# Seven half-size products for the second FFN layer of the last three token tiles, and a residue-first attention output

## The chip, the cores and the metric

The kernel runs on one core of a Trainium2 chip. The metric is device time in microseconds (us). Before the change three runs took 296.37, 297.34 and 298.47 us; the median, 297.34 us, is the time that the change is compared with. Five engines work beside each other, each in the order of its own instruction list, and wait for each other by semaphores: TensorE (PE for its matmuls, PEld for its weight loads), VectorE (DVE), ScalarE (ACT), GpSimd (POOL) and SyncE (SP). SP and POOL mainly issue DMAs here.

## The reference

A masked attention (8 batches, 8 heads, 576 positions, head size 64) feeds a feed-forward layer with squared ReLU over 8 x 576 = 4608 tokens.

```python
mask_plain = (rel >= 0) & (rel < window)                                             # heads 0-3
mask_dil = (rel >= 0) & (rel < window * dilation) & (rel % dilation == 0)            # heads 4-7
attn = softmax(where(mask, scale * q @ k.T, -1e9));  attn_out = attn @ v             # window 32, dilation 4
x = attn_out.transpose(0, 2, 1, 3).reshape(4608, 512)
h = np.maximum(x @ w_in, 0.0)                                                        # w_in 512 x 2048
out = h * h @ w_out                                                                  # w_out 2048 x 512
```

## The kernel before

All matmuls take bf16 operands and add up in float32. The attention output is kept transposed in `xT`, 128 channels on the partitions and four blocks of channels (`KT`), in a ring of four batches. Positions are held by residue modulo 4 (`RES`), since the dilated heads look only at positions of their own residue: within a batch the 576 columns stand as 4 residues x 144.

The FFN goes over the tokens in tiles: four tiles of 256 tokens, then seven of 512, which this text numbers 2 to 8 (tile t begins at token 512 t). `ffn_groups` gives the PE work of a tile as a list of small functions. The first half, `g1`, is the first layer: for each of the 16 blocks of 128 hidden features (`NF`) four matmuls over the channel blocks (L971), 128 x 128 weights against 512 columns of `xT`, into one PSUM bank of the pool `ps_f` (four banks, used in turn; the profile calls them `pf`). ACT then takes the ReLU from the bank into `h2T` (L984) and DVE squares it in place (L987). The second half, `g2`, is the second layer: for each of the four blocks of 128 tokens sixteen matmuls (L1027) with a block of `h2T` as the weights and 512 columns of `w_out` streaming; a copy takes the bank to `osb` (L1033, ACT as a rule), and `store` issues it to DRAM on SP's queue (L941). `store` cuts a block of 128 rows wherever a residue ends, so a block goes out in one to three pieces. In the very last block the columns are cut 384 + 128, so that the last copy and the last store are short.

`h2T` is a fresh 512-token buffer for each tile, from a pool of two.

The attention of a batch is laid between the groups of the FFN, with an order written by hand: `PROGRAM` for the first batches, and for the later ones a list `steps` of (group, order, batch, code), with the group number g at which a step is issued. A 512-token tile has 32 groups (`G`), 16 of g1 and 16 of g2. For batch 7, the last, two visits of PE remain in tile 6: after its group 15 (scores of two head pairs, and the products with v of the two others) and after its group 23 (products with v of the last two). Around them ACT takes the exponentials (code E, L730), DVE multiplies by the mask (L732) and adds neighbouring pieces (L735, L744), ACT forms the reciprocal row sums as exp(-ln d) (codes L and X, L698 to L713), and DVE multiplies the result into `xT` (L716, L720). After that, tiles 7 and 8 hold FFN work alone.

Loads of q, k and v go over POOL's queue; `rb[0..2]` are the staging buffers of q and k. `rb[0]` and `rb[2]` are last used by batches 2 and 3.

Of the kernel before, what the change touches and what calls it, by code (L numbers as in the profile page):

```python
# [12 lines left out]
RES = 4  # L13
# [50 lines left out]
def kernel(  # L64
# [9 lines left out]
    nc = tc.nc  # L74
# [3 lines left out]
    NTOK = B * S  # L78
# [30 lines left out]
    h2_pool = ctx.enter_context(tc.tile_pool(name="h2", bufs=2))  # L109
# [26 lines left out]
    rb = [{nm: const.tile([(80, P, 80)[i], 2 * H * RES * D], bf16, name=f"{nm}b{i}") for nm in "qk"} for i in range(3)]  # L136
# [9 lines left out]


    v_rows = [t[:, 0:2, :, :].rearrange("p e i c -> p (e i c)").rearrange("p (e i d) -> p e i d", e=NE, d=D) for t in vbd]
    q_both = qT[:, :, :, :]
    k_both = kbd[:, 0:2, :, :].rearrange("p e i c -> p (e i c)").rearrange("p (i h t) -> p i h t", i=NB, h=NE)  # L150
    ends = [
# [205 lines left out]
    def byr(ap):  # L357
        return ap.rearrange("p (r m) -> p r m", r=RES)
# [165 lines left out]
    def batch1(code: str):  # L524
# [140 lines left out]
        else:  # L665
            e = int(code[1])
            es = (e, e + 1) if part == 0 else (e,)
            if what == "l":
                two["r", e] = rec = r_pool.tile([P, 576], f32, name="rec")
                for x, e in enumerate(es):  # L670
                    ds = two["o", e, part][1]
                    to = rec[:, w * x : w * x + w]
                    if len(ds) == 1:
                        nc.scalar.activation(to, ds[0], ACT.Ln)
                        continue
                    to = to.rearrange("p (c j m) -> p j c m", c=2, j=2)
                    for j, d in enumerate(ds):
                        nc.scalar.activation(to[:, j, :, :], d.rearrange("p (c m) -> p c m", c=2), ACT.Ln)
            else:
                rec = two.pop(("r", e))[:, 0 : w * len(es)]  # L680
                nc.scalar.activation(rec, rec, ACT.Exp, scale=-1.0)
                t0 = S % RING + RES * m0
                for x, e in enumerate(es):
                    o, _ = two.pop(("o", e, part))
                    nc.vector.tensor_tensor(out=xT[:, e, t0 : t0 + w], in0=o, in1=rec[:, w * x : w * x + w], op=ALU.mult)

    def natural_step(b: int, code: str):
        what, e = code[0], int(code[1])
# [21 lines left out]
        elif what == "X":  # L710
            o, _, rest = op.pop((b, e))
            rec = recs.pop((b, e))
            nc.scalar.activation(rec[:, :], rec[:, :], ACT.Exp, scale=-1.0)  # L713
            t0 = b * S % RING
            tok = byr(xT[:, e, t0 : t0 + S])
            nc.vector.tensor_tensor(out=tok[:, :, 16:M], in0=byr(o[:, :]), in1=byr(rec[:, 0:512]), op=ALU.mult)  # L716
            for g, rows in enumerate(sides) if rest[0][0] is not rest[0][1] else [(0, slice(0, P))]:
                if rest[0][0] is not rest[1][0]:
# [49 lines left out]
    def first_step(code: str):  # L768
# [128 lines left out]
        elif what == "D":  # L897
            dms = first.pop(("D", e, part))
            for x, (dd, rh) in enumerate(dms):
                nc.tensor.matmul(  # L900
                    dd, ones[:, :], rh, start=(x == 0 and y0 == 0), stop=(x == len(dms) - 1), skip_group_check=True
                )
        else:
            n = 512 if part == 0 else w
            if what == "L":
                first["X", e, part] = rec = r_pool.tile([P, 576], f32, name="rec")
                nc.scalar.activation(rec[:, 0:n], first["P", e, part][1][:, 0:n], ACT.Ln)
            elif what == "X":
                rec = first["X", e, part][:, 0:n]
                nc.scalar.activation(rec, rec, ACT.Exp, scale=-1.0)  # L910
            else:
                o, rec = first["P", e, part][0][:, 0:n], first.pop(("X", e, part))[:, 0:n]
                to = xT[:, e, RES * m0 : RES * m0 + n]
                if part == 0:
                    to = xT[:, e : e + 2, 0:w]
                    o, rec = [x.rearrange("p (e n) -> p e n", e=2) for x in (o, rec)]
                nc.vector.tensor_tensor(out=to, in0=o, in1=rec, op=ALU.mult)

    def attention_steps(b: int, base: int, at):
# [6 lines left out]
        return out  # L926


    def store(osb, pos: int, c0: int, c1: int, cuts=None):

        x = 0
        while x < P:
            b, y = divmod(pos + x, S)
            part = int(y >= RES * MN[0]) if b in PARTED else 0
            w = MN[part] if b in PARTED else M
            r, m = divmod(y - RES * MS[part], w)
            n = min(P - x, w - m)
            row = b * S + RES * (MS[part] + m) + r
            at = cuts(n) if cuts else (c0, c1)
            for y0, y1 in zip(at, at[1:]):  # L940
                nc.sync.dma_start(out[row : row + RES * (n - 1) + 1 : RES, y0:y1], osb[x : x + n, y0:y1])  # L941
            x += n

    def ffn_groups(tk0: int, nt: int):

        early = NT <= tk0 <= 3 * NT
        h2 = h2_pool.tile([P, NF, NT], bf16, name="h2T")
        per = NT // nt  # L950
        kts = (2, 0, 3, 1) if tk0 > 3 * NT else (2, 3, 1, 0) if tk0 == 2 * NT else (0, 1, 2, 3) if tk0 == 0 else (2, 3, 0, 1)
        cur, acc = {}, {}

        half = nt // 2
        over = tk0 // RING != (tk0 + nt - 1) // RING
        assert not over or (tk0 + half) % RING == 0

        def mm1(u, ks):
            if u not in acc:
                acc[u] = ps_f.tile([P, NT], f32, name="pf")  # L960
            for x in range(per):
                f = per * u + x
                piece = max(y for y in range(len(w_in_sb)) if w_cuts[y] <= P * f)
                c0 = 512 * (f // 4) + f % 4 - w_cuts[piece]
                for kt in ks:
                    t0 = tk0 % RING
                    to, rhs = acc[u][:, nt * x : nt * x + nt], xT[:, kt, t0 : min(t0 + nt, RING)]
                    if over:
                        to = to.rearrange("p (a t) -> p a t", a=2)
                        rhs = xT[:, kt, :].rearrange("p (a t) -> p a t", t=half)[:, 0 : t0 // half + 1 : t0 // half, :]  # L970
                    nc.tensor.matmul(  # L971
                        to,
                        w_in_sb[piece][:, kt, c0 : c0 + 509 : 4],
                        rhs,
                        start=(kt == kts[0] and x == 0),
                        stop=(kt == kts[-1] and x == per - 1),
                        skip_group_check=True,
                    )
            if ks[-1] != kts[-1]:
                return  # L980
            hv = h2[:, per * u : per * u + per, 0:nt]

            def relu():
                nc.scalar.activation(hv, acc[u][:, :].rearrange("p (x n) -> p x n", x=per), ACT.Relu)  # L984

            def square():
                nc.vector.tensor_tensor(out=hv, in0=hv, in1=hv, op=ALU.mult)  # L987

            def floor():
                nc.vector.tensor_scalar(  # L990
                    out=hv, in0=acc[u][:, :].rearrange("p (x n) -> p x n", x=per), scalar1=0.0, scalar2=None, op0=ALU.max
                )

            if tk0 == 0 and u < 2:
                held.append((floor if u else relu, square))
            else:
                relu()
                square()

        def g1(i):  # L1000
            if i < 2 and tk0 < NT or i < 6 and tk0 == 0:
# [17 lines left out]
        def g2(m, part):  # L1019
# [11 lines left out]
            if f1 == NF:  # L1031
                osb = osb_pool.tile([P, DM], f32, name="osb")
                (nc.vector.tensor_copy if last and part == 1 or tk0 == 3 * NT // 2 else nc.scalar.copy)(osb[:, c0:c1], cur[m][:, c0:c1])  # L1033
                pos = tk0 + (P * m + half) % nt if over else tk0 + P * m
                if tk0 == NTOK - NT and m in (0, 2):
                    store(osb, pos, c0, c1, lambda n: (c0, DM // 2, c1) if m == 0 or n > P // 2 else (c0, c1))
                else:
                    store(osb, pos, c0, c1)
# [77 lines left out]
    def cross_all(b):  # L1116
        for part in range(2):
            for nm in "kq":
                cross(b, nm, part)

    def run(code):
        if code == "y":
# [181 lines left out]
```

## Time and profile before

| what | value |
|---|---|
| median of three runs | 297.34 us (296.37 to 298.47) |
| span of the profiled execution, first to last instruction | 294.1 us |
| busy: PE / PEld | 286.2 us (97%) / 165.8 us (56%) |
| busy: ACT / DVE / POOL | 187.2 us (64%) / 155.5 us (53%) / 123.2 us (42%) |
| PE in the first layer (L971) | 127.6 us |
| PE in the second layer (L1027) | 126.0 us |
| tile 6 in the span | 205.08 to 234.91 us |
| tile 7 | 234.91 to 262.54 us |
| tile 8, then the last copies and stores | 262.54 to 294.1 us |

Of the profiled execution the profile gives the span; its own time as a run isn't recorded beside it. The median of the timed runs is 3.2 us above the span: what lies before the first and behind the last instruction of the span, and the difference between one execution and another. In the rows below, times such as "start us" count from the span's start, "mean ns of one" is the recorded length of one instruction (matmuls overlap in the array, so the distance from start to start is what a matmul costs), and the arrow in brackets names what an engine waited for.

### The profile page before, as it was taken

The page shows a single profiled execution, that of the slowest core. Times are in us where ns is not written, and L with a number is a line of the kernel's source. Part 1 is how long each engine was busy: PE and PEld are TensorE (multiplying, and loading weights), DVE is VectorE, ACT ScalarE, POOL GpSimd, SP SyncE. Part 2 cuts the span into 40 slices and gives each one's busy share as a digit, 9 for nine tenths or more (in the row PEclk, how much of TensorE's full clock was granted, in tenths as well). Part 3 has the DMA queues.
Part 4 walks back from the last instruction along what each step waited for, and adds up shares of the span by engine and source line. Part 5 has one row for each costly group of instructions (what it writes and reads, how often), then busy time and mean ns, then how long its engine had stood idle before and what let it go on. Part 6 is the DMA issues. An engine that isn't in the chain of part 4 may idle for free.

```text
span 294.1 us, 7899 instructions
## 1 busy us (share of the span) xinstructions
PE 286.2 (97%) x3213; PEld 165.8 (56%) x3241; DVE 155.5 (53%) x452; ACT 187.2 (64%) x381; POOL 123.2 (42%) x208
## 2 busy tenths in 40 slices
PE   8999999999999999999999999999999999999994
PEld 6689647859555554555455545554554455445443
DVE  2785224647779566685659465947454245004300
ACT  6888545887667774988567656766676476127411
POOL 8686266847626965776763696000000000000000
PEclk9999999999999999999999999999999999999999
DMA  8999999999999999999999698012101210121022
GB/s 120 199 188 214 203 225 197 193 169 190 162 230 141 140 157 199 138 159 171 179 176 116 97 170 144 2 37 73 36 2 39 71 38 0 37 74 33 0 71 71
DMA packets 84211, 35.75 MB, mean 122 GB/s; under 512 B 53600, under 2 KB 79424, under 8 KB 84176
## 3 DMA queue, kind: packets, MB, share of 16 engines
q0 software_dynamic: 49056, 18.49, 56.5%
q1 hardware_dynamic: 34976, 16.67, 28.0%
q8 instruction: 25, 0.41, 0.6%
q10 hardware_dynamic: 144, 0.10, 0.1%
q14 instruction: 10, 0.08, 0.1%
HBM read 37.50 MB, written 9.44 MB: 160 GB/s over the span
## 4 chain that ended last, share of the span: by engine, by line
PE 93%; ACT 1%; issue 1%; DMA 1%; DVE 1%; POOL 0%; ACTq 0%; POOLq 0%
PE pf L1027 42%; PE pf L971 41%; PE po L369 2%; PE pa L369 2%; PE pf L369 1%; DMA kb<-in_k_dram 1%; ACT h2T L984 1%; PE pa L794 1%; PE pd L369 1%; PE pf L846 1%; DVE h2T L987 1%; PE po L764 1%; PE pa L564 0%; DVE qT L335 0%; PE po L884 0%
## 5 line engine op out<-in xcount | busy, mean ns | idle before, releaser
L971 PE MATMUL pf<-xT,w_in 128*128 128x512 bf16 (+1 forms) x697 | 127.6, 340 | 0.4
L1027 PE MATMUL pf<-w_out_sb,h2T 128*128 128x512 bf16 (+2 forms) x571 | 126.0, 373 | 1.6 <-issue 0.6
L984 ACT ACTIVATE h2T<-pf 128x512 bf16<-128x512 f32 x143 | 83.9, 600 | 32.3 <-PE pf L971 32.0
L971 PEld LDWEIGHTS <-w_in 128*128 128x128 bf16 x704 | 78.0, 113 | 46.3 <-issue 0.3
L987 DVE TENSOR_TENSOR h2T<-h2T 128x512 bf16<-128x512 bf16 x144 | 60.0, 424 | 61.5 <-ACT h2T L984 59.6
L1027 PEld LDWEIGHTS <-h2T 128*128 128x128 bf16 x592 | 56.1, 98 | 63.9
L321 POOL DMA_DIRECT2D vbd<-in_v_dram x80 | 43.5, 560 | 23.6 <-DMA kb<-in_k_dram 9.7
L1033 ACT COPY osb<-pf 128x512 f32<-128x512 f32 (+1 forms) x34 | 19.5, 574 | 50.5 <-PE pf L1027 50.5
L175 POOL DMA_DIRECT2D qb<-in_q_dram x19 | 13.7, 722 | 8.3 <-DMA xx<-qb 4.6
L713 ACT ACTIVATE rec<-rec 128x576 f32<-128x576 f32 x24 | 16.4, 683 | 0.7
L175 POOL DMA_DIRECT2D kb<-in_k_dram x19 | 13.3, 698 | 5.8 <-DMA w_in<-in_moe_w_in_dram 1.9
L197 POOL DMA_DIRECT2D vbd<-in_v_dram x16 | 11.0, 687 | 8.9 <-DMA kb<-in_k_dram 5.3
L730 ACT ACTIVATE pt<-pa 128x384 bf16<-128x384 f32 (+1 forms) x26 | 11.7, 498 | 4.5 <-DVE xT L720 3.8
L307 POOL DMA_DIRECT2D vd<-in_v_dram x20 | 12.0, 615 | 3.2 <-PE pa L369 2.1
L313 POOL DMA_DIRECT2D vbd<-in_v_dram x20 | 12.0, 618 | 3.2 <-PE pf L369 1.9
L716 DVE TENSOR_TENSOR xT<-pf,rec 128x512 bf16<-128x512 f32 x11 | 7.6, 692 | 10.5 <-ACT rec L713 10.5
L716 DVE TENSOR_TENSOR xT<-po,rec 128x512 bf16<-128x512 f32 x13 | 9.0, 691 | 6.5 <-ACT rec L713 6.3
L732 DVE TENSOR_TENSOR pt<-pt,mask_n 128x384 bf16<-128x384 bf16 (+1 forms) x20 | 7.2, 374 | 8.6 <-ACT pt L730 8.5
L732 DVE TENSOR_TENSOR pt<-pt,mask_f 128x384 bf16<-128x384 bf16 x24 | 8.4, 355 | 6.1 <-ACT pt L730 5.9
L369 PEld LDWEIGHTS <-vbd 64*64 64x64 bf16 x328 | 8.4, 107 | 4.4 <-issue 4.0
L337 DVE COPY qT<-xx 64x576 bf16<-64x576 bf16 (+1 forms) x30 | 10.5, 351 | 0.6
L730 ACT ACTIVATE pt<-pf 128x448 bf16<-128x448 f32 (+1 forms) x18 | 8.6, 519 | 1.0 <-PE pf L369 0.9
(156 smaller groups left out, 280.5 us busy)
## 6 DMA issues: line engine op xcount, KB each, us to landing
qb<-in_q_dram POOLq DMA_DIRECT2D x7, 320.0 KB, 6.8
kb<-in_k_dram POOLq DMA_DIRECT2D x7, 320.0 KB, 8.0
vd<-in_v_dram POOLq DMA_DIRECT2D x34, 64.0 KB, 4.5
w_out_sb<-in_moe_w_out_dram POOLq DMA_DIRECT2D x4, 512.0 KB, 13.0
out_dram<-osb SPq DMA_DIRECT2D x16, 128.0 KB, 5.0
qb<-in_q_dram POOLq DMA_DIRECT2D x6, 256.0 KB, 6.4
kb<-in_k_dram POOLq DMA_DIRECT2D x6, 256.0 KB, 8.8
out_dram<-osb SPq DMA_DIRECT2D x9, 160.0 KB, 3.7
```

The costliest lines, as they stand in the source:

```text
L175: nc.gpsimd.dma_start(t[p0 : p0 + n, part, h0:h1, :], src[b, h0:h1, t0 : t0 + RES * n, :].rearrange("h (p r) d -> p h (r d)", r=RES),)
L321: nc.gpsimd.dma_start(v_rows[b % 2][p0 + 16 * r : p0 + 16 * r + 16, e, :, :], v[b, 2 * e + hl, :, :].rearrange("(i m r) d -> r m i d", r=R ...
L369: nc.tensor.matmul(out, lhs, rhs, start=begin, stop=True, skip_group_check=True)
L713: nc.scalar.activation(rec[:, :], rec[:, :], ACT.Exp, scale=-1.0)
L716: nc.vector.tensor_tensor(out=tok[:, :, 16:M], in0=byr(o[:, :]), in1=byr(rec[:, 0:512]), op=ALU.mult)
L730: nc.scalar.activation(pt, sp[b, e][g][:, 0:n], ACT.Exp, scale=SCALE)
L732: nc.vector.tensor_tensor(out=pt, in0=pt, in1=mask, op=ALU.mult)
L971: nc.tensor.matmul(to, w_in_sb[piece][:, kt, c0 : c0 + 509 : 4], rhs, start=(kt == kts[0] and x == 0), stop=(kt == kts[-1] and x == per - ...
L984: nc.scalar.activation(hv, acc[u][:, :].rearrange("p (x n) -> p x n", x=per), ACT.Relu)
L987: nc.vector.tensor_tensor(out=hv, in0=hv, in1=hv, op=ALU.mult)
L1027: nc.tensor.matmul(cur[m][:, c0:c1], h2[:, f, P * m : P * m + P], w_out_sb[:, f, c0:c1], start=(f == 0), stop=(f == NF - 1),)
L1033: (nc.vector.tensor_copy if last and part == 1 or tk0 == 3 * NT // 2 else nc.scalar.copy)(osb[:, c0:c1], cur[m][:, c0:c1])
```

## The change

**Second layer of tiles 6, 7 and 8** (`FAST = 6`). The 512 tokens, 2048 features and 512 output columns are each cut in two. The output quarters c11, c12, c21, c22 then come from seven products of half size instead of eight: M1 to M7, each 8 feature blocks x 2 token blocks of 128 x 256 columns, so 16 matmuls of 256 columns, 112 in a tile (L1110 of the changed kernel) where there were 64 of 512. Four of the products use sums of quarters of `h2T` or of `w_out`:

- `add_up` (L1032) forms four sums of quarters of the squared `h2T` on DVE, one of them in place, in three portions after feature steps 7, 11 and 15 of g1 (1024, 512 and 512 elements to a partition each). They lie in `rb[2]`.
- `weigh` (L1258) forms four sums of quarters of `w_out`, in eight DVE instructions of 1024 elements, one after each of groups 1 to 8 of tile 5. They lie in `rb[0]`.
- The features of g1 are taken in the order 0, 8, 1, 9, ..., and the squares (L996) are taken in pairs of 1024 elements, but for the last two.
- `after` puts the products together. ACT copies bank X to `snap0` behind M1 (L1052); M6 then goes on adding in the same bank X, and ACT copies it again behind M6 (L1058). DVE adds banks and earlier sums into `whole`, float32, 128 x 512 to an instruction (`plus`, L1039): one each behind M2, M4, M7 and M3, two behind M5. The order on PE is M1, M2, M6, M4, M7, M5, M3.
- In tiles 6 and 7 `keep` stores two rows of blocks behind M5 and two behind M3. In tile 8 it stores halves: two stores behind each of M2, M7 and M5, and M3 comes in three pieces (256, 128 and 128 columns) with a `plus` and a store each.

**Residue-first `xT`.** `xT` is now 4 residues x 576 for the whole ring, and a tile of 512 tokens is 4 runs of 128 columns, a block of 128 outputs one residue: `store` writes it in one piece (two where a tile crosses the end of the ring).

**One `h2T`** for all tiles, in place of a pool of two; 256-token tiles use its halves in turn.

The order of the instructions on POOL is the same in both kernels. On PE, ACT and DVE it is the same but for the shapes up to tile 5, where the eight `weigh` instructions stand in DVE's list, and from tile 6's squares on.

```diff
-    PARTED = (0, 1)
+    FAST = 6
...
-    xT = const.tile([P, KT, RING], bf16, name="xT")
+    xT = const.tile([P, KT, RES, RING // RES], bf16, name="xT")
...
+    h2T = const.tile([P, NF, NT], bf16, name="h2T")
+    snap = [const.tile([P, 2, HD], f32, name=f"snap{x}") for x in range(2)]
+    whole = const.tile([P, 4, DM], f32, name="whole")
...
-        h2 = h2_pool.tile([P, NF, NT], bf16, name="h2T")
+        h2 = h2T[:, :, at : at + nt]
+        fast = tk0 >= FAST * NT
...
+                        to, rhs = to.rearrange("p (r m) -> p r m", r=RES), xT[:, kt, :, t0 : t0 + nm]
...
+            if not fast or u >= NF - 2:
                 square()
+            elif u % 2:
+                hv = h2[:, u // 2 : u // 2 + NF // 2 + 1 : NF // 2, :]
+                square()
+            if fast and u in sums_at:
+                add_up(*sums_at[u])
+
+        sums_at = {7: (0, 4), 11: (4, 6), 15: (6, 8)}
...
+            for to, one, two_, op in (
+                (s1, a21, a22, ALU.add),
+                (a21, a11, a21, ALU.subtract),
+                (s2, s1, a11, ALU.subtract),
+                (s4, a12, s2, ALU.subtract),
+            ):
+                nc.vector.tensor_tensor(out=to, in0=one, in1=two_, op=op)
...
+            if name == "M1":
+                nc.scalar.copy(snap[0][:, :, :], bank["X"])
+            elif name == "M2":
+                plus(c11, bank["Z"], snap[0][:, :, :])
...
+            elif name == "M6":
+                nc.scalar.copy(snap[1][:, :, :], bank["X"])
+            elif name == "M4":
+                plus(c21, bank["W"], snap[1][:, :, :])
+            elif name == "M7":
+                plus(c21, bank["V"], c21)
...
+            elif name == "M5":
+                plus(snap[0][:, :, :], bank["Y"], snap[1][:, :, :])
+                plus(c22, bank["V"], snap[0][:, :, :])
+                keep((1, 3), *((HD, DM) if final else (0, DM)))
+            elif not final:
+                plus(c12, bank["Q"], snap[0][:, :, :])
+                keep((0, 2), 0, DM)
...
+            "M1": ("X", raw(0, 0), w_raw(0, 0)),
+            "M2": ("Z", raw(1, 0), w_raw(1, 0)),
+            "M6": ("X", summed(1), w_of(1)),
+            "M4": ("W", raw(1, 1), w_of(3)),
+            "M7": ("V", raw(0, 1), w_of(2)),
+            "M5": ("Y", summed(0), w_of(0)),
+            "M3": ("Q", summed(2), w_raw(1, 1)),
...
+                begin = f == 0 and (piece or i == 0) and name != "M6"
+                if begin:
+                    cur[bank] = ps_f.tile([P, 2, HD], f32, name="pf")
...
+                if piece:
+                    plus(c12[:, i, y0:y1], cur[bank][:, i, y0:y1], snap[0][:, i, y0:y1])
+                    keep((2 * i,), HD + y0, HD + y1)
...
+        nc.vector.tensor_tensor(out=order[y][0], in0=order[y][1], in1=order[y][2], op=ALU.subtract)
...
+        if G * (FAST - 1) < g <= G * (FAST - 1) + 8:
+            weigh(g - G * (FAST - 1) - 1)
```

More of the change, by code (lines that the diff above doesn't have):

```diff
@@ L980, in mm1 @@
                 return
-            hv = h2[:, per * u : per * u + per, 0:nt]
+            hv = h2[:, f0 : f0 + per, :]
             def relu():
@@ new lines, in ffn_groups, with plus, keep @@
+        final = tk0 + nt == NTOK
+        kept = whole[:, :, :].rearrange("p (i j) c -> p j i c", j=2)
+        c11, c12, c21, c22 = (kept[:, j, :, HD * y : HD * y + HD] for j in range(2) for y in range(2))
+        def plus(to, one, two_):
+            nc.vector.tensor_tensor(out=to, in0=one, in1=two_, op=ALU.add)
+        def keep(rows, *cuts):
+            for m in rows:
+                parts = [(0, half, tk0 + m + RES * half), (half, half, tk0 + m)] if over else [(0, P, tk0 + m)]
+                store(whole[:, m, :], parts, *cuts)
@@ L1119, in cross_all, with weigh @@
                 cross(b, nm, part)
+    def weigh(x):
+        y, f = divmod(x, 2)
+        fs, gs = slice(4 * f, 4 * f + 4), slice(NF // 2 + 4 * f, NF // 2 + 4 * f + 4)
+        b11, b12, b21, b22 = (w_out_sb[:, z, c : c + HD] for z in (fs, gs) for c in (0, HD))
+        to = [w[:, fs, :] for w in w_sum]
+        order = (
+            (to[0], b12, b11),
+            (to[2], b22, b12),
+            (to[1], b22, to[0]),
+            (to[3], b21, to[1]),
+        )
+        nc.vector.tensor_tensor(out=order[y][0], in0=order[y][1], in1=order[y][2], op=ALU.subtract)
     def run(code):
```

121 lines of the change are left out of this document (85 added, 36 removed).

## The prediction, made before the changed kernel ran

> **What bounds the kernel now.** First the page: its shares, the granted clock and the chain that ended last.
>
> ```profile
> span 294.1 us, 7899 instructions
> PE 286.2 (97%) x3213; PEld 165.8 (56%) x3241; DVE 155.5 (53%) x452; ACT 187.2 (64%) x381; POOL 123.2 (42%) x208
> PEclk9999999999999999999999999999999999999999
> PE 93%; ACT 1%; issue 1%; DMA 1%; DVE 1%; POOL 0%; ACTq 0%; POOLq 0%
> ```
>
> PE is busy for 97% of the span at an even clock, and 93% of the last chain is PE's. A microsecond off PE's list is a microsecond off the time, as long as no other engine comes late. Who could come late is read from the stages that the change touches, busy time by engine (columns: stretch, length, PE, PEld, DVE, ACT, POOL, clock, DMA):
>
> ```profile
> 205.08:218.98 13.90, 13.85 (x64) 7.14 (x63) 6.25 (x16) 9.54 (x16) 0.00 (x0) 1.00 0.06 19
> 218.98:234.91 15.93, 15.83 (x229) 8.12 (x231) 6.05 (x17) 9.19 (x20) 0.00 (x0) 1.00 0.17 52
> 234.91:248.73 13.82, 13.77 (x65) 7.23 (x65) 5.99 (x15) 9.54 (x16) 0.00 (x0) 1.00 0.06 20
> 248.73:262.54 13.81, 13.71 (x63) 6.26 (x64) 0.81 (x2) 2.35 (x4) 0.00 (x0) 1.00 0.19 57
> 262.54:276.35 13.81, 13.76 (x64) 7.23 (x64) 5.99 (x15) 9.54 (x16) 0.00 (x0) 1.00 0.09 20
> 276.35:294.10 17.75, 13.97 (x80) 7.15 (x79) 1.38 (x3) 2.62 (x5) 0.00 (x0) 1.00 0.20 59
> ```
>
> These are first and second layer of tiles 6, 7 and 8. PE fills each; DVE has 6 of 13.8 us to do in a first layer and next to nothing in a second, except in tile 6, where attention still runs.
>
> **Term 1, the products.** A second layer is 64 matmuls of 512 columns: 13.81 us by tile 7's row, 0.216 each. It becomes 112 of 256 columns, each with a weight load of its own. What such a matmul costs, the early tiles show, whose first layer has 256 columns; from PE's timeline:
>
> ```profile
> 22.45 9.78 PE L971 MATMUL pf<-xT,w_in 128*128 128x256 bf16 x88
> 32.06 7.07 PE L1027 MATMUL pf<-w_out_sb,h2T 128*128 128x512 bf16 x31
> 144.64 13.98 PE L971 MATMUL pf<-xT,w_in 128*128 128x512 bf16 x64
> 174.86 13.98 PE L971 MATMUL pf<-xT,w_in 128*128 128x512 bf16 x63
> ```
>
> 88 of them go from 22.45 to 32.06: 9.61 / 88 = 0.1092 us, weight loads included. So 112 x 0.1092 = 12.23 us, and a tile gains 13.82 - 12.23 = 1.59 us, three tiles **4.77 us**. Tile 8 ends in 8 pieces of 256 and 16 of 128 columns in place of 16 of 256; 16 matmuls of 128 lie between the starts of the last two copies (289.57 and 290.45 below), 0.88 / 16 = 0.055 us, just half of 0.109, so nothing is lost there. The upper bound for a 256-column matmul is the mean over all early ones, switches to attention and back among them:
>
> ```profile
> L971 PE MATMUL pf<-xT,w_in 128*128 128x256 bf16 x256 | 29.6, 273 | 0.0
> L971 PEld LDWEIGHTS <-w_in 128*128 128x128 bf16 x704 | 78.0, 113 | 46.3 <-issue 0.3
> ```
>
> 29.6 / 256 = 0.1156 us makes 12.95 us a tile and 2.6 us of gain in all. I take 0.1092, since the products come in long runs. The Trainium skill (TensorE: Matmul & The Clock Gate, Back-to-back issue gap) speaks against this step: it says that in a stream of load and matmul pairs both set the spacing, 81 ns at 128 columns where the matmul alone takes 56. An estimate with those extra 25 ns on each of 112 makes 15.0 us a tile, slower than now. The two rows above (55 ns at 128 columns, 109 at 256, a load to each) do not agree, so the sum goes without it.
>
> The residue-first `xT` makes the streamed operand of the first layer 4 runs of 128 columns. The tile at 144.64 already reads two runs apart, across the end of the ring, and takes 13.98 us like the plain one at 174.86. I take nothing for it; half a per cent of the first layers, 0.6 us, would be the most that two equal rows leave open. The single `h2T` adds waits of a ReLU on readers that stand before its own matmuls in PE's list or a tile earlier in DVE's: nothing, covered by PE's order.
>
> **Term 2, DVE's new work.** A bf16 instruction with two inputs, by the groups:
>
> ```profile
> L987 DVE TENSOR_TENSOR h2T<-h2T 128x512 bf16<-128x512 bf16 x144 | 60.0, 424 | 61.5 <-ACT h2T L984 59.6
> L732 DVE TENSOR_TENSOR pt<-pt,mask_f 128x384 bf16<-128x384 bf16 x24 | 8.4, 355 | 6.1 <-ACT pt L730 5.9
> L744 DVE TENSOR_TENSOR kbd<-pt 128x128 bf16<-128x128 bf16 x12 | 2.7, 225 | 0.4
> L716 DVE TENSOR_TENSOR xT<-po,rec 128x512 bf16<-128x512 f32 x13 | 9.0, 691 | 6.5 <-ACT rec L713 6.3
> ```
>
> (424 - 355) / 128 = 0.54 ns an element; 128 elements in runs of eight (L744) cost 225 ns, on the same line, so runs do not cost the rate. 1024 elements then take 424 + 512 x 0.54 = 0.70 us, and where the next need not wait for the result 0.62, since an instruction may begin 0.08 us before the end of the one ahead (L716 and L720 in tile 6 below: 0.69 long, 0.61 apart). Nothing before shows 1024 elements in one instruction; below the line there is no reason, above it the bound is twice the slope, 1.25 us. I take 0.70.
>
> `weigh`: eight of 0.62 to 0.70 in tile 5's first layer, one to each 0.86 us step.
>
> ```profile
> 182.59 0.42 DVE L987 TENSOR_TENSOR h2T<-h2T 128x512 bf16<-128x512 bf16 x1 [0.44 <-ACT h2T L984]
> 187.47 0.46 DVE L339 COPY kbd<-xx 64x256 bf16<-64x256 bf16 x2
> 189.50 0.42 DVE L987 TENSOR_TENSOR h2T<-h2T 128x512 bf16<-128x512 bf16 x1
> 189.96 7.08 PE L1027 MATMUL pf<-w_out_sb,h2T 128*128 128x512 bf16 x31
> 195.33 0.21 DVE L720 TENSOR_TENSOR xT<-pa,rec 128x64 bf16<-128x64 f32 x1
> ```
>
> DVE rests 0.44 us a step, so it falls behind by up to 8 x 0.26 = 2.1 us and, filled further on with the arranging of q and k (the copies of 187.47, no rest before them), stays so. The last square then ends at 189.92 + 2.1 = 192.0; PE needs that feature after 15 matmuls, at 189.96 + 15 x 0.216 = 193.2. The attention work behind it, done at 195.5, has gaps to swallow part of the delay, and PE's next visit is at 197.0. Hidden: **0**. At 1.25 us each the cover would be gone and some 4 us lost.
>
> Tiles 7 and 8: pairs of squares (7 x 0.70), two single ones and twelve sums (4 x 0.70 and 8 x 0.42) make about 12 us of 13.8, and M1 and M2, which need no sums, cover the last portion with 3.5 us. **0**, though with little to spare at M1's last feature (rival 2).
>
> Tile 6 is different, because attention's DVE work stands behind the sums and M6 behind attention:
>
> ```profile
> 212.81 0.42 DVE L987 TENSOR_TENSOR h2T<-h2T 128x512 bf16<-128x512 bf16 x1 [0.44 <-ACT h2T L984]
> 219.09 0.60 ACT L984 ACTIVATE h2T<-pf 128x512 bf16<-128x512 f32 x1 [0.27 <-PE pf L971]
> 220.16 0.74 DVE L732 TENSOR_TENSOR pt<-pt,mask_n 128x448 bf16<-128x448 bf16 x2
> 221.86 0.69 DVE L716 TENSOR_TENSOR xT<-pf,rec 128x512 bf16<-128x512 f32 x1 [0.58 <-ACT rec L713]
> 222.47 0.21 DVE L720 TENSOR_TENSOR xT<-pa,rec 128x64 bf16<-128x64 f32 x1
> 222.71 0.87 ACT L730 ACTIVATE pt<-pa 128x384 bf16<-128x384 f32 x2 [0.89 <-DVE xT L720]
> 223.47 0.60 ACT L698 ACTIVATE rec<-pd 128x512 f32<-128x512 f32 x1
> 220.18 7.08 PE L1027 MATMUL pf<-w_out_sb,h2T 128*128 128x512 bf16 x31
> ```
>
> The eighth ReLU is ready at 212.8. From there DVE has eight instructions of 1024 and ten of 512 elements before the first mask: 8 x 0.62 + 10 x 0.34 = 8.4 us if none waits for another, 8 x 0.70 + 10 x 0.42 = 9.8 if each does, and it is not before the last ReLU (219.7), a square and a portion of sums: 221.4. That gives 221.4 to 222.6; about half of the sums wait, so 222.1 in place of 220.16. From mask to the end of L720 it is 222.68 - 220.16 - 0.58 (a rest that vanishes) = 1.94 us: 224.0. The two exponentials of L730 begin 0.03 us behind L720, and the changed kernel has the same wait there. ACT comes free 223.47 - 222.71 = 0.76 us later, and only then, next in its list, stands the copy of bank X (0.58 us by the like copy of 512 columns): 225.4. M6 adds into that bank and must wait for it. Without a wait M6 would begin at 220.18 + 32 x 0.109 = 223.67. PE stands for **1.75 us** (1.1 to 2.3), in tile 6 alone; behind M6 wait M4, the second visit and everything after. In tiles 7 and 8 ACT is free and the copy (0.6 us) hides behind M2 (1.75 us).
>
> **Term 3, the end.** SP issues of the last tile, and the last copies:
>
> ```profile
> 287.57 0.79 SPq L941 DMA_DIRECT2D out_dram<-osb  x2
> 288.40 0.45 SPq L941 DMA_DIRECT2D out_dram<-osb  x1
> 289.57 0.56 DVE L1033 COPY osb<-pf 128x384 f32<-128x384 f32 x1 [11.96 <-DMA out_dram<-osb]
> 290.45 0.27 ACT L1033 COPY osb<-pf 128x128 f32<-128x128 f32 x1 [2.91 <-PE pf L1027]
> 290.74 0.35 SPq L941 DMA_DIRECT2D out_dram<-osb  x1
> ```
>
> Now the last store is issued 0.29 us after the last copy may start (290.45), and 3.36 us before the span's end. Call the moment R at which the last piece's `plus` may start. M5 was done 1.75 us before R; its two `plus` (0.69 each, the second needing the first) end at R - 0.33. SP then issues two stores for them and three for M3's pieces. Three issues back to back start 287.57 to 288.40, 0.41 us apart, so the fifth starts at R - 0.3 + 4 x 0.41 = R + 1.3 in place of R + 0.29: **1.0 us** lost. If SP took no time, DVE's list alone would end near R + 0.35 (0.1 lost); 1.3 is the other bound. The earlier stores and the fewer, larger pieces lie under PE's work.
>
> **Sum.** -4.77 + 1.75 + 1.0 = -2.0 us against the span of 294.1, so 292.1. The runs' median lies 3.2 us above the span; with the same distance the changed kernel takes **295.3 us**, 0.7% faster. Best ends: -4.77 + 1.1 + 0.1 = -3.6 (293.8). Worst: -2.6 + 2.3 + 1.3 + 0.6 = +1.6 (298.9).
>
> **Rivals.**
> 1. *Full gain.* The copy of bank X is not held up, or hardly (DVE's sums overlap better, or ACT's order lets it through): 297.34 - 4.77 + 1.0 = 293.6, and 292.7 if SP's issues hide too. For it: ACT and DVE have slack on average. Against: the 0.89 us wait of the exponentials on DVE stands in the row. 25%.
> 2. *DVE becomes the bound* (slower than before). The place is the square of feature step 14, which M1's last feature needs 13.82 + 14 x 0.109 = 15.3 us into a tile. From the eighth ReLU, 212.8 - 205.1 = 7.7 us into it, DVE has before that square four pairs of squares (0.62 each), four sums of 1024, four of 512 and the square: with x for 1024 and 0.6 x for 512 elements 2.6 + 6.4 x, overlaps taken off, so x = 0.8 is the point from which M1 comes late in tiles 7 and 8, while in tile 6 the held copy goes by 8.8 x. At 1.25 us it is 3.0 us late in tiles 7 and 8, 1.8 in tile 6 (behind the visit), and the held copy is 3 us later still: 295.3 + 6.0 + 1.8 + 3 = 306; the gain is gone near 0.85. Against: L744 on the line. 8%.
> 3. *The change does not do what it says.* At 0.1156 us a matmul the gain is 2.6 us and terms 2 and 3 take 2.75: 297.5, no change. At 0.123 (13.82 / 112) the products gain nothing and the kernel is 2.8 us slower, 300.1. Against: 88 matmuls at 0.1092. 10%, a third of it beyond 1%.
> 4. *Loads not hidden.* Were each load of 0.113 us to stand beside its matmul, 112 x 0.222 = 24.9 us a tile and 333 in all. Against: the same 88. 1%; the skill's rule above is a mild form of it.
>
> **How the numbers follow.** My case has 56%; its own range, from the bounds of terms 2 and 3, is 294.0 to 296.6. With rivals 1 and 3 the range is 293.3 to 298.0, which leaves out part of 1, all of 2 and 4, and the far part of 3. A measurement of this kernel tells about 1% from no change. Faster by over 1% (under 294.4): rival 1 and a fifth of my case's edge, 30%. Slower by over 1%: rivals 2 and 4 and part of 3, 13%. Within 1%: 57%.
>
> **What would show it.** In the changed trace: L1110 with starts 0.109 us apart and 12.2 us a tile in tiles 7 and 8; in tile 6 one idle time of PE of 1 to 2.5 us behind M2, put down to ACT's copy (L1052); DVE's sums near 0.70 and 0.42 us; tile 5 unchanged at 30.2 us; the last five issues of SP about 0.4 us apart. A first layer above 14 us would make the free strides wrong, an idle PE at M1 of tiles 7 and 8 DVE's rate, and no idle PE in tile 6 would make term 2 wrong.

## The result

The changed kernel takes **293.99 us** (median of 16 runs, 293.29 to 296.26), the kernel before, run beside it, 296.41 us (median of 16, 295.56 to 298.47). The ratio is **0.992 (95% interval 0.991 to 0.994)**, 2.3 us or 0.8% faster: a small gain that is certain in sign and lies inside the "within 1%" of the forecast. Forecast were 295.3 us, against a median before of 297.34.

The page of the changed kernel: span, busy shares, the chain that ended last.

```profile
span 292.4 us, 8216 instructions
PE 282.7 (97%) x3361; PEld 179.7 (61%) x3377; DVE 183.5 (63%) x494; ACT 184.4 (63%) x375; POOL 123.2 (42%) x208
PE 88%; DVE 5%; DMA 2%; ACT 2%; issue 1%; POOL 1%; DVEq 0%; POOLq 0%
```

PE's recorded work is 3.5 us less (286.2 before, where the page lacks some matmul records: 697 of 704 in the first layer), DVE's 28 us more (155.5), and DVE's part of the last chain rises from 1% to 5%. The span fell by only 1.7 us. Where it went is read from PE's timeline, tile 6 to the end:

```profile
23.23 9.78 PE L980 MATMUL pf<-xT,w_in 128*128 128x256 bf16 x88
205.92 13.98 PE L980 MATMUL pf<-xT,w_in 128*128 128x512 bf16 x64
221.03 3.67 PE L1110 MATMUL pf<-w_out_sb,h2T 128*128 128x256 bf16 x32
226.16 1.91 PE L1110 MATMUL pf<-qb,qb 128*128 128x256 bf16 x16 [1.46 <-ACT snap L1052]
235.79 13.98 PE L980 MATMUL pf<-xT,w_in 128*128 128x512 bf16 x64
249.61 3.66 PE L1110 MATMUL pf<-w_out_sb,h2T 128*128 128x256 bf16 x32
261.83 13.98 PE L980 MATMUL pf<-xT,w_in 128*128 128x512 bf16 x64
286.13 1.93 PE L1110 MATMUL pf<-w_out_sb,kb 128*128 128x256 bf16 x24
```

The page rounds the span; the stretch from 288.08 to its end shows it to 0.01 us (stretch, length, engines):

```profile
288.08:292.36 4.28, 0.00 (x0) 0.00 (x0) 0.39 (x2) 0.00 (x0) 0.00 (x0) 0.97 0.38 123
```

Against the starts of before (205.08, 234.91, 262.54, and R, the moment when the last copy may start, 290.45; now 286.13 plus 8 x 0.109 and 16 x 0.055 for M3's pieces, plus the 0.2 us by which the sums follow PE's rows, 288.08):

| Stretch | before | after | change |
|---|---|---|---|
| span start to tile 6 | 205.08 | 205.92 | +0.84 |
| tile 6 | 29.83 | 29.87 | +0.04 |
| tile 7 | 27.63 | 26.04 | -1.59 |
| tile 8 to R | 27.91 | 26.25 | -1.66 |
| R to the span's end | 3.65 | 4.28 | +0.63 |

The first line is for the most part not the change's doing: the run of 88 matmuls starts at 23.23 in place of 22.45, so 0.78 of the 0.84 is there before the first weight difference is made, and further on the distances are those of before. This opening, in which PE waits for loads and copies, differs from one execution to the next: the same row starts between 22.71 and 24.47 in the runs below, and at 27.98 in one execution of the changed kernel. The earliest start with the whole change in place is 22.72, so at most 0.3 us of it could be the change's. Without this line the sum is -2.6 us, and the runs say -2.3.

So two tiles gained what the products save, tile 6 gained nothing, and the end gave back 0.63. The second layers by engine (stretch, length, PE, PEld, DVE, ACT, POOL, clock, DMA):

```profile
249.61:261.83 12.22, 12.22 (x113) 10.96 (x112) 6.66 (x13) 1.77 (x3) 0.00 (x0) 1.00 0.01 1
275.65:292.40 16.75, 12.41 (x121) 11.06 (x119) 7.44 (x16) 1.77 (x3) 0.00 (x0) 0.99 0.19 63
```

Tile 7's takes 12.22 us (13.81 before), at the granted clock of before, and PE is busy for all of it, with 112 loads taking 10.96 us beside it. In tile 6 PE stands idle ahead of M6. The rows of DVE and ACT there:

```profile
222.96 0.65 DVE L742 TENSOR_TENSOR pt<-pt,mask_n 128x448 bf16<-128x448 bf16 x2
224.50 0.22 DVE L730 TENSOR_TENSOR xT<-pa,rec 128x64 bf16<-128x64 f32 x1
224.75 0.87 ACT L740 ACTIVATE pt<-pa 128x384 bf16<-128x384 f32 x2 [2.07 <-DVE xT L730]
225.51 0.59 ACT L1052 COPY snap<-pf 128x512 f32<-128x512 f32 x1
```

The last sums end, the masks start at 222.96; ACT's two exponentials wait 2.07 us for DVE's L730; the copy of bank X, ready for ACT since M1 ended near 222.8, follows at 225.51; M6, next in PE's list at 221.03 + 32 x 0.109 = 224.52, starts at 226.16. Held: 1.64 us.

### The profile page after: what moved, and what is told of

The parts are those of the page before. It is cut to its first block, busy times and chain, and to the rows that moved or that the text cites. A ratio compares the mean times of both kernels' runs of the same rounds, so it can differ in the third digit from the quotient of the medians.

```text
span 292.4 us, 8216 instructions
## 1 busy us (share of the span) xinstructions
PE 282.7 (97%) x3361; PEld 179.7 (61%) x3377; DVE 183.5 (63%) x494; ACT 184.4 (63%) x375; POOL 123.2 (42%) x208
## 4 chain that ended last, share of the span: by engine, by line
PE 88%; DVE 5%; DMA 2%; ACT 2%; issue 1%; POOL 1%; DVEq 0%; POOLq 0%
PE pf L980 39%; PE pf L1148 28%; PE pf L1110 11%; DMA kb<-in_k_dram 2%; PE po L377 2%; DVE h2T L996 2%; PE pa L377 1%; PE pf L377 1%; DVE qb L1032 1%; ACT h2T L993 1%; PE pd L377 1%; PE pa L804 1%; ACT pt L740 1%; DVE kb L1032 1%; PE pf L856 0%
## 5 line engine op out<-in xcount | busy, mean ns | idle before, releaser
L1148 PE MATMUL pf<-w_out_sb,h2T 128*128 128x512 bf16 x368 | 84.1, 379 | 1.4 <-issue 0.6
L996 DVE TENSOR_TENSOR h2T<-h2T 128x512 bf16<-128x512 bf16 (+1 forms) x123 | 55.9, 468 | 33.4 <-ACT h2T L993 31.7
L1148 PEld LDWEIGHTS <-h2T 128*128 128x128 bf16 x384 | 36.5, 98 | 42.3
L1154 ACT COPY osb<-pf 128x512 f32<-128x512 f32 x22 | 12.9, 585 | 20.8 <-PE pf L1148 20.8
L1110 PEld LDWEIGHTS <-h2T 128*128 128x128 bf16 x192 | 18.6, 98 | 2.6
L726 DVE TENSOR_TENSOR xT<-po,rec 128x512 bf16<-128x512 f32 x13 | 9.0, 691 | 6.9 <-ACT rec L723 6.6
L1039 DVE TENSOR_TENSOR whole<-pf,snap 128x512 f32<-128x512 f32 (+2 forms) x14 | 8.2, 612 | 7.9 <-PE pf L1110 7.8
L1110 PE MATMUL pf<-qb,qb 128*128 128x256 bf16 x96 | 11.5, 272 | 1.5 <-ACT snap L1052 1.5
L726 DVE TENSOR_TENSOR xT<-pf,rec 128x512 bf16<-128x512 f32 x11 | 7.6, 691 | 7.6 <-ACT rec L723 7.6
```

The lines of the kernel that those rows point to most:

```text
L1110: nc.tensor.matmul(cur[bank][:, i, y0:y1], lhs(f, i), rhs(f)[:, y0:y1], start=begin, stop=f == NF // 2 - 1, skip_group_check=True)
L1148: nc.tensor.matmul(cur[m][:, c0:c1], h2[:, f, P * m : P * m + P], w_out_sb[:, f, c0:c1], start=(f == 0), stop=(f == NF - 1),)
```

## The experiments

The theory: the products give their full 1.59 us a tile; tile 6 loses it again because ACT's copy of bank X stands in ACT's list behind exponentials that DVE's sums make late; the end loses because SP issues five stores one after the other. The rivals: M6 waits for its sums; the loss in tile 6 is attention's own; the layout of `xT` takes part; the end is set by the data. All ratios are to the kernel before, in runs on the same chip, with 95% intervals.

**The changed kernel again.**

> The changed kernel once more, beside the three variants below on one chip. Expected: 0.992 of the time before, and again a PE hold of about 1.6 us ahead of M6 in tile 6.

0.9927 (0.9899 to 0.9954), as expected, and the hold is there again: PE stands idle 1.46 us ahead of M6, just as above. The profiled execution was one of 302.44 us with a span of 300.7; all of the 8.3 us that it is longer lie ahead of tile 6 (which starts at 214.22 in place of 205.92), and 4.75 of them ahead of the run of 88 matmuls. A row of it is used in the last section.

**The copy ahead of the exponentials.**

```diff
-            expo(3, t + 16, t + 16)
+            expo(3, *[t + 16 + (b > FAST)] * 2)
```

> Tile 6's last two exponentials (E30, E31) are issued one step later, so ACT's copy of bank X stands ahead of them in ACT's list; nothing else moves. Theory: M6 is held only because that copy stands behind exponentials that wait for DVE; the copy then runs at M1's end (about 222.8 us on the changed kernel's clock), M6 begins without a wait, and the time falls by 1.6 us against the changed kernel (ratio to before 0.987). Rival: M6 waits for its sums from DVE; then the hold stays at 1.4 us or more and the ratio at 0.992. A third outcome: the exponentials, now later, hold the second visit, and PE's wait only moves there: 0 to -0.5 us.

**0.9855 (0.9836 to 0.9874)**. Timeline of this kernel, tile 6:

```profile
220.99 3.67 PE L1110 MATMUL pf<-w_out_sb,h2T 128*128 128x256 bf16 x32
222.95 0.59 ACT L1052 COPY snap<-pf 128x512 f32<-128x512 f32 x1 [0.31 <-PE pf L1110]
224.50 1.91 PE L1110 MATMUL pf<-qb,qb 128*128 128x256 bf16 x16
224.72 0.87 ACT L740 ACTIVATE pt<-pa 128x384 bf16<-128x384 f32 x2 [1.18 <-DVE xT L730]
234.14 13.98 PE L980 MATMUL pf<-xT,w_in 128*128 128x512 bf16 x64
```

The exponentials still start at 224.72, since they wait for DVE either way; the copy now runs in the time that ACT spent waiting, and M6 has no wait. Tile 6 takes 234.14 - 205.89 = 28.25 us, 1.62 less, nearly all of the 1.64 held. M6's operand sums were ready in time, so the rival of late sums falls.

**M4 between M2 and M6.** In the list of products M4 comes ahead of M6, and its sum into c21 is made behind M6's copy:

```diff
+            "M4": ("W", raw(1, 1), w_of(3)),
             "M6": ("X", summed(1), w_of(1)),
-            "M4": ("W", raw(1, 1), w_of(3)),
```

> The products run in the order M1, M2, M4, M6, M7, M5, M3 in all three tiles, so M4 (1.75 us, its own bank) lies between M2 and M6. Theory: the copy of bank X is done 1.5 us after M2 in tile 6, M4 covers that, and the time falls by 1.5 to 1.6 us against the changed kernel (ratio 0.987). This covers late sums as well, so it does not tell the theory from the rival by itself; if the wait does not go, neither is right and it is the bank rotation or the second visit.

0.9872 (0.9853 to 0.9891). M6 starts at 226.22 without a wait, as expected, but tile 6 saves 1.19 us, not 1.5. The copy keeps its old place behind the exponentials, so attention's normalisation behind it on ACT is as late as in the changed kernel, and now PE, early, meets it. Timeline of this kernel:

```profile
227.41 0.69 DVE L726 TENSOR_TENSOR xT<-po,rec 128x512 bf16<-128x512 f32 x1 [1.19 <-ACT rec L723]
228.02 0.21 DVE L730 TENSOR_TENSOR xT<-pa,rec 128x64 bf16<-128x64 f32 x1
228.16 0.39 PE L377 MATMUL po<-pt,vbd 64*64 64x96 bf16 x2
```

The second visit's first pair goes into the bank that L726 reads. L726 ends at 228.10, the pair spreads over 0.39 us and its successors start at 228.37; in the kernel with the copy ahead, ACT reaches that normalisation earlier and the visit has no such wait. Covering a wait leaves what is queued behind it late; taking away its cause does not.

**Part of the sums behind the masks.** In tile 6 alone the last portion of sums is issued two steps of the second layer later:

```diff
-            if fast and u in sums_at:
+            if fast and u in sums_at and not (u == 15 and tk0 == FAST * NT):
...
+            if n == 2 and tk0 == FAST * NT:
+                add_up(*sums_at[15])
```

> In tile 6 the last four sums (4 of 512 elements, 1.6 us of DVE) are issued behind attention's masks and normalisation, not ahead of them; everything else as in the changed kernel. Theory: DVE's sums make the exponentials late, so these start 1.6 us earlier (at about 223.1 us in place of 224.75), the copy of bank X ends near 224.5 and the hold of M6 falls from 1.64 to 0 to 0.3 us (ratio 0.987); M6's own sums, now ending near 224.6, may keep up to 0.3 us of it. Rival: the exponentials wait for something else in attention (PE's visit, the normalisation by ACT); then the hold stays above 1 us (ratio 0.991).

0.987 (0.984 to 0.990). Timeline of this kernel:

```profile
223.50 0.87 ACT L740 ACTIVATE pt<-pa 128x384 bf16<-128x384 f32 x2 [0.89 <-DVE xT L730]
224.25 0.59 ACT L1052 COPY snap<-pf 128x512 f32<-128x512 f32 x1
224.90 1.92 PE L1112 MATMUL pf<-qb,qb 128*128 128x256 bf16 x16 [0.27 <-ACT snap L1052]
```

The exponentials start 1.25 us earlier, with the wait of 0.89 us that the kernel before has, the copy moves with them, and the hold falls from 1.64 to 0.45 us (224.90 against 220.96 + 32 x 0.109). DVE's sums are what made the exponentials late. The 0.45 left, a little over what was expected, still ends with ACT's copy. M6's own sums were later than expected, the one that it reads done at 226.15, but only M6's last four matmuls need that portion, from 226.2 on. With the run that puts the copy ahead, both links of the chain are shown: sums to exponentials, exponentials to copy.

**Only the layout.** `FAST = 99`: no products, no weight differences.

> No tile takes the seven products, and no weight differences are made: left of the change are the residue-first xT and the single h2T. Theory: they cost nothing, ratio 1.000 within 0.001, first layers 13.98 us in the timeline as before, tile 5 30.2 us. Rival: the streamed operand in four runs, or the ReLU's waits on h2T's readers, cost part of the gain; then 0.3 to 0.6 us slower (ratio 1.001 to 1.002), in the first layers.

1.0008 (0.9987 to 1.0029). Tile 5 takes 30.22 us, tile 6 29.84, tile 7 27.63, each as before. The residue-first `xT` and the single `h2T` cost nothing that the trace shows; the interval alone would leave up to 0.9 us open. The end is even 0.2 us shorter, 3.44 us from R in place of 3.65, so measured from this kernel the products' end loses 0.84 us.

**Only tiles 7 and 8.** `FAST = 7`.

> Only tiles 7 and 8 take the seven products; tile 6 runs its eight as before, and the weight differences move to tile 6's first layer. Theory: tile 6 won 1.59 us and lost 1.64 to the hold, so leaving it out changes nothing against the changed kernel (ratio 0.991 to 0.993). Rival: the hold of tile 6 only uses up slack that the attention there has anyway; then the time is 1.6 us above the changed kernel's (ratio 0.997).

0.9931 (0.9904 to 0.9957), the same as with three tiles. Timeline of this kernel:

```profile
207.39 13.98 PE L980 MATMUL pf<-xT,w_in 128*128 128x512 bf16 x64
237.23 13.98 PE L980 MATMUL pf<-xT,w_in 128*128 128x512 bf16 x64
263.27 13.98 PE L980 MATMUL pf<-xT,w_in 128*128 128x512 bf16 x64
```

Tile 6 with its old products takes 29.84 us, with the new ones 29.87; tile 7 takes 26.04 in both. Tile 6's part of the change is worth nothing as it stands.

**One more sum.** Each portion writes its first sum once more, to an unused buffer:

```diff
+                (spare, a21, a22, ALU.add),
                 (s1, a21, a22, ALU.add),
```

> Each portion of sums writes its first sum once more to an unused buffer: one DVE instruction of 1024 and two of 512 elements more in each of tiles 6, 7 and 8 (0.62 to 0.72 and 0.35 to 0.45 us each); the rest is the changed kernel. Theory: DVE stands 0.27 us ahead of M1's last features in tiles 7 and 8, so 1.0 us more of DVE work ahead of that square makes PE wait 0.7 us in each; in tile 6 the hold of M6 grows by all three, 1.3 to 1.5 us. Together 2.7 to 2.9 us over the changed kernel, ratio to before 1.001 to 1.003. Rival: DVE has idle time in those layers (6 of 13.8 us busy before) and swallows the work; then only tile 6 loses, 0.997, or nothing does, 0.992.

**1.006 (1.003 to 1.009)**, some 4 us over the changed kernel, more than either side said. Timeline, then stretches of tile 6 with the clock as the last but two column:

```profile
226.61 0.59 ACT L1055 COPY snap<-pf 128x512 f32<-128x512 f32 x1
227.25 3.34 PE L1113 MATMUL pf<-qb,qb 128*128 128x256 bf16 x16 [2.73 <-ACT snap L1055]
254.05 2.48 PE L1113 MATMUL pf<-w_out_sb,h2T 128*128 128x256 bf16 x20 [0.44 <-DVE h2T L996]
280.89 2.47 PE L1113 MATMUL pf<-w_out_sb,h2T 128*128 128x256 bf16 x20 [0.50 <-DVE h2T L996]
```

```profile
227.25:228.80 1.55, 1.55 (x8) 1.11 (x8) 0.36 (x2) 1.25 (x3) 0.00 (x0) 0.50 0.04 11
228.80:230.43 1.63, 1.63 (x10) 1.18 (x9) 1.19 (x3) 0.00 (x0) 0.00 (x0) 0.56 0.00 0
230.43:232.00 1.57, 1.57 (x17) 1.40 (x15) 0.00 (x0) 0.59 (x1) 0.00 (x0) 1.00 0.00 0
```

Tiles 7 and 8 wait for DVE's square at M1's last features and take 0.73 and 0.79 us more: the slack there was as small as said, and DVE's idle time on average swallows nothing. The hold of M6 grows by 1.3 us to 2.9, as said. What was not expected is the next 3 us: behind this hold PE is granted a clock of 0.50, and M6's 16 matmuls take 3.18 us (227.25 to 230.43) in place of 1.74. 0.73 + 0.79 + 1.3 + 1.4 make 4.2.

**Four tiles.** `FAST = 5`, with the later exponentials and the stores of the next experiment.

> The seven products in tile 5 too (weight differences in tile 4's first layer), with the exponentials one step later in tiles 5 and 6 and M5's last stores on ACT's queue. Theory: tile 5's attention leaves DVE no room: its second layer has 11.8 us of DVE work in 16.4 already, 4.1 us of sums into f32 come on top while PE's part shrinks to 14.8; so DVE makes PE wait 1 to 2.5 us in tile 5 or at tile 6's first visit, and the fourth tile's 1.59 us are gone: 0.985 to 0.990. Rival: mean slack of DVE counts; then 1.6 us faster than with three tiles, 0.981.

1.0008 (0.9983 to 1.0032): all of the gain is gone. Timeline of this kernel in tile 5:

```profile
178.65 1.67 PE L980 MATMUL pf<-xT,w_in 128*128 128x512 bf16 x7
196.26 0.39 PE L1110 MATMUL pf<-w_out_sb,h2T 128*128 128x256 bf16 x2 [1.02 <-DVE h2T L996]
204.70 0.43 PE L377 MATMUL po<-pt,vbd 64*64 64x96 bf16 x2 [2.26 <-DVE xT L726]
212.84 2.32 PE L980 MATMUL pf<-xT,w_in 128*128 128x512 bf16 x10
```

Tile 5 takes 34.2 us in place of 30.2. PE waits 1.2 us for the squares of M1, then 2.3 us for attention's normalisation, and behind that wait it runs at half its clock for 3.41 us (rows in the last section). The direction was expected, the size (1 to 2.5 us of waiting) was not: the waits come to 3.5 us, and the slow clock, by an estimate of half of 3.41, adds 1.7. DVE, 65% busy over this span, sets PE's pace in that tile.

**The last stores.** First M5's two last stores on ACT's queue, with the changed kernel otherwise; then this with the later exponentials ("best"); then also the middle one of M3's three on ACT:

```diff
-                keep((1, 3), *((HD, DM) if final else (0, DM)))
+                keep((1, 3), *((HD, DM) if final else (0, DM)), by=nc.scalar if final else nc.sync)
```

> In the last tile the two stores of M5's rows are issued by ACT's queue, so SP issues only M3's three pieces at the end. Theory: SP's five issues in a row, 0.47 us apart, set the end; the last one then starts 0.8 to 1.0 us earlier and the time falls by 0.6 to 0.9 us (ratio 0.990). Rival: the end is set by the data and the DMA engines, or by DVE's list (its last sum ends at 288.47 us, 0.35 before SP's fourth issue); then at most 0.2 us.

> Both edits that helped: the two exponentials one step later and M5's last two stores on ACT's queue. Theory: they act in different places, one in tile 6 and one behind the last product, so their gains add: 1.65 and 0.37 us against the changed kernel's span, ratio 0.984 to 0.985. Rival: what ends the program is the landing of the last data, and the earlier issue gains nothing more; then 0.9855 as with the first edit alone.

> The exponentials one step later, M5's last two stores and the middle one of M3's three on ACT's queue: SP issues two at the end, and the last of them can start where its sum ends, R + 0.45 in place of R + 0.95. Theory: the issues in a row set the end, span end at R + 3.5 to 3.65, 0.3 to 0.5 us less than with two stores on ACT (R + 4.0). Rival: the landing of the last data sets it (the stores lie in each other's way on the DMA engines); then R + 3.9 to 4.0.

0.9902 (0.9886 to 0.9919), 0.9866 (0.9834 to 0.9897) and **0.9851 (0.9836 to 0.9865)**. SP's issues of the changed kernel, then the two queues of the first variant, whose clock is 0.43 us ahead:

```profile
287.77 0.81 SPq L944 DMA_DIRECT2D out_dram<-whole  x2
288.16 0.92 SPq L944 DMA_DIRECT2D out_dram<-whole  x2
288.68 0.89 SPq L944 DMA_DIRECT2D out_dram<-whole  x2
289.17 0.89 SPq L944 DMA_DIRECT2D out_dram<-whole  x2
```

```profile
287.35 0.86 ACTq L944 DMA_DIRECT2D out_dram<-whole  x2
288.60 0.40 SPq L944 DMA_DIRECT2D out_dram<-whole  x1
```

Neighbouring rows share an issue: the five of the changed kernel start at 287.77, 288.16, 288.68, 289.17 and, by the last row's end, 289.66, 0.47 us apart. On two queues the last starts at 288.60, 0.63 us earlier after the 0.43, but the end comes only 0.3 us earlier, at R + 3.99 (best: R + 4.00) in place of R + 4.28; the 0.37 in the second expectation came from spans rounded to 0.1 us. With three on ACT and two on SP the end is at R + 3.88, where the theory said 3.5 to 3.65 and the rival 3.9 to 4.0. So about half of the loss is the issues in a row.

The traces also hold the landings: from the last landing to the span's end it is 0.99 us in all four, but from the start of the last issue to its landing it is 1.71 us in the changed kernel, 2.04 in the first variant, 2.06 in best and 2.23 with three on ACT. The landing eats up much of what the earlier issue gains, which is in part what the rival said. What makes it later was not told apart.

In the runs, the last two do not differ by more than their intervals from the later exponentials alone (0.9855); that the gains add is shown by the traces only, where R to the end is 4.28 us with the later exponentials alone and 4.00 and 3.88 with the stores split as well.

The fastest version here is the last, 291.89 us against 296.36 beside it: 1.5% faster than before, some 2 us faster than the changed kernel.

## Why the prediction was right, and where not

**The products (term 1): right.** Predicted 0.1092 us a matmul and 12.23 us a layer; 12.22 in tiles 7 and 8. The upper bound of 0.1156 was a mean over switches and did not apply. The rule of the Trainium skill (TensorE: Matmul & The Clock Gate, Back-to-back issue gap) that a load beside each matmul adds 25 ns at 128 columns would have made 15.0 us by the prediction's estimate; the trace does not agree. That layout and `h2T` cost nothing was right too (the layout alone).

**DVE's prices (term 2): right.** 1024 elements take 0.69 us (0.70 said, 21 squares at a mean of 689 ns), 512 elements 0.42.

```profile
L996 DVE TENSOR_TENSOR h2T<-h2T 128x1024 bf16<-128x1024 bf16 x21 | 14.2, 689 | 15.0 <-ACT h2T L993 15.0
```

Tile 5, which starts with this row, takes 205.92 - 175.70 = 30.22 us with `weigh`, as predicted:

```profile
175.70 13.98 PE L980 MATMUL pf<-xT,w_in 128*128 128x512 bf16 x64
```

**The hold in tile 6 (term 2): right, step by step.** On the clock of before (0.84 us earlier): first mask 222.12 (222.1 said), L730 done 223.88 (224.0), copy done 225.26 (225.4), hold 1.64 us (1.75). Rival 1, the copy that is not held up, did not come by itself; moving two exponentials in ACT's list brought it.

**The end (term 3): mis-sized.** 0.63 us, not 1.0. The step that failed is the silent one: that the 3.36 us from the last issue to the span's end stay the same. The last issue did start late, at R + 1.6 (said: R + 1.3; the issues were 0.47 us apart, not 0.41), but the end followed 2.7 us behind it. Before, 2.07 us lay between the start of that issue and its landing and 1.30 behind the landing; now it is 1.71 and 0.99. The 0.3 us saved behind the landing are SP's: it passes seven waits there in the kernel before and two in the changed one, 0.06 us apart. Why the landing itself came sooner stays open.

**Rival 2, DVE as the bound: its place was right, and it was nearer than its 8% sounds.** M1's last features had 0.27 us to spare in tiles 7 and 8: in tile 7 they are due at 249.61 + 14 x 0.109 = 251.14, and the square of step 14, behind a pair that starts at 249.84, ends at 249.84 + 0.61 + 0.42 = 250.87. One more sum a portion cost 1.5 us at this place in the two tiles.

```profile
249.84 0.69 DVE L996 TENSOR_TENSOR h2T<-h2T 128x1024 bf16<-128x1024 bf16 x1
```

**The time: the base was mis-sized.** 295.3 was 1.3 us too high, although the span of 292.1 was near (292.36 measured, 0.84 of it the later opening). The 3.2 us that the prediction laid on top, from the span to the runs' median, don't fit the runs: where time and span of one execution are both on record here, they lie 1.8 to 2.1 us apart (294.17 and 292.36 for the changed kernel). By that the profiled execution of before took, as an estimate, some 296 us, less than any of the three runs whose median was the base, and the sixteen runs of the kernel before have a median of 296.41, not 297.34. By parts, the change was predicted at -4.77 + 1.75 + 1.0 = -2.0 us, and the terms as measured give -4.77 + 1.64 + 0.63 = -2.5, against -2.3 in the runs and -2.6 in the trace without the opening.

**The range: partly luck.** 293.99 lies inside the whole range but just below the one given for the case itself, 294.0 to 296.6. That one does not follow from its own bounds: these make -3.6 and, at the other end, -4.77 + 2.3 + 1.3 = -1.2 us, so 293.8 to 296.2. By the time alone rival 1, with its 293.6, would have looked the better forecast. What decides against it is the hold of 1.64 us in the trace and that it went away with one edit, not the number of 293.99.

## What to carry to other kernels

Where an engine with idle time gets work ahead of a chain of another engine's waits, follow the chain to the end: the cost fell on a copy that needed neither DVE nor attention, only ACT's place in line. Then put the ready instruction ahead of the one that waits: here that cost nothing and was worth 1.6 us, as much as the change won in a whole tile. And an average share of 63% says little of an engine whose work must be done between two events: 0.27 us was all the slack there was.

## What the runs showed of the hardware

An idle PE can cost more than its idle time, since the granted clock may fall behind it. It falls in steps: in the three traces where it falls while PE has work, it is 0.50 for 3.41 us and then 1.00 again, and every stretch of full clock between two falls is a whole number of such steps. The rows are of the run with four tiles, of the second profiled execution of the changed kernel (and its longest wait), and of its first, one step to a row:

```profile
201.51:204.92 3.41, 1.14 (x13) 0.73 (x11) 2.09 (x8) 2.63 (x6) 0.00 (x0) 1.00 0.00 0
204.92:208.33 3.41, 3.41 (x108) 2.97 (x109) 2.14 (x6) 2.18 (x5) 0.00 (x0) 0.50 0.02 5
```

```profile
71.44:74.85 3.41, 1.49 (x28) 1.04 (x28) 1.40 (x5) 0.90 (x2) 3.07 (x5) 1.00 1.86 121
74.85:78.26 3.41, 3.38 (x34) 2.49 (x34) 1.07 (x3) 1.19 (x4) 1.77 (x3) 0.50 1.42 207
78.26:81.67 3.41, 3.41 (x33) 3.37 (x31) 2.64 (x8) 3.24 (x7) 0.59 (x1) 1.00 1.64 128
73.53 0.34 PE L377 MATMUL pa<-xx 64*64 64x80 bf16 x16 [1.17 <-DMA xx<-qb]
```

```profile
223.84:227.25 3.41, 1.95 (x19) 1.59 (x18) 1.82 (x7) 2.46 (x6) 0.00 (x0) 1.00 0.02 5
227.25:230.66 3.41, 3.41 (x89) 2.92 (x87) 2.11 (x4) 0.78 (x2) 0.00 (x0) 1.00 0.00 0
```

The length of one idle time does not decide: in the second group the longest was 1.17 us and the clock fell, in the third one of 1.46 us left it alone. What sorts these cases is PE's idle time added up over the step before: 2.27 us (3.41 - 1.14), 1.92 and, in one more sum from 223.40 to 226.81, 2.29 us were followed by 0.50; 1.46 was not. Behind PE's last work it is the same: 1.57 us in a step left the clock at 1.00 (two stores on ACT's queue), 2.04 brought it to 0.50 (part of the sums behind the masks). If that is what counts, the place of a wait among the steps matters as well as its length. A slow step costs up to half of its length, 1.7 us by this estimate.

The Trainium skill (TensorE: Matmul & The Clock Gate, Part 1: The HAM clock gate) has this mechanism: half the clock after an idle window of about 3.4 us, full clock after a window busy for about as long. The halving and the length of a step agree with these rows; a step idle throughout was not needed, as 1.92 of 3.41 us was enough here. Its advice (Why this matters for your kernels) to have no gaps of over about 3 us was too generous in this kernel.

That idle times of 1.57 and 1.92 us bracket the point does not make it a fixed one: neither the length nor the place of a wait was varied by itself.
